# Output units of a group started inside the group: lightning attention with an ACT-snake MLP on one core

## Chip, core and metric

The kernel runs on one core of a Trainium2 chip. The metric is the device time of one execution in microseconds; the time before is the median of three runs, 215.41 us (215.19 to 215.55). One further execution was taken by the hardware profiler. Its own time was 215.56 us, and every duration below is from it, in us from the start of its span.

## What is computed

A causal linear attention with decay (4 batches, 8 heads, 768 positions, head size 64), whose output, as 3072 tokens of 512 columns, goes through an MLP: `h = x @ w_in` (2048 columns), `g = h + sin(alpha h)^2 / alpha`, `out = g @ w_out`.

```python
for b in range(nb):                      # blocks of 64 positions
    intra = einsum('bhic,bhjc->bhij', qb, kb) * Dmask
    intra = einsum('bhij,bhjd->bhid', intra, vb)
    inter = einsum('bhid,bhde->bhie', qb * lam_pow, kv_state)
    out[:, :, sl] = intra + inter
    kv_state = lam_block * kv_state + einsum('bhsd,bhse->bhde', kb * rev_pow, vb)
x = out.transpose(0, 2, 1, 3).reshape(3072, 512)
h = x @ w_in
s = sin(alpha * h)
g = h + s * s / (alpha + 1e-09)
result = g @ w_out
```

## The kernel before

**Tiling.** The 768 positions are cut into NT = 6 chunks of 128. A group g is the MLP of chunk g for all four batches, 512 tokens. The attention of chunk g+1 runs inside the loop of group g, so that its matmuls, its VectorE work and its loads lie between the MLP's.

**The loop.** `for g in range(1, NT + 1)` (L615) has 16 steps i. Each step does, in this order: the loads and transposes that `feed(g)` lists for i; `hidden(g, i)`, which is four matmuls of 128x512 (L402) into a PSUM bank, then the sine on ScalarE (L405) and, where `squarer` says ScalarE, the square (L408); the attention parts that `slots(g)` lists for i; `run(1)`, which takes one unit from the list `behind`; `finish(g, i)`, which is the square on VectorE where `squarer` says so (L416) and then `gall[:, i] = s2 * r + h` from the bank (L417). Group 6 has no hidden parts; it only empties `behind`. At the very end `project_halves` computes the last row block.

**Units.** The second matmul, `g @ w_out`, has four row blocks m (one batch each), and each is four parts of four matmuls (`project`, L427): 16 units for a group, 12 for the last, whose fourth block is `project_halves`. Part p reads the columns f = 4p to 4p+3 of `gall[g]`. Before the change a group's units are queued behind its loop (L636), so they run within the next group's steps, one to a step. Part 0 of a block opens a PSUM bank (L424): for groups 1 to 3 always bank 3 (`OB`), for groups 4 and 5 banks 3 and 4 in turn. Part 3 ends with `store`: a copy from the bank to memory on chip, by VectorE for groups 1 to 3 (L434) and by ScalarE otherwise (L436), and a store on SP's queue (L438).

**Which steps run a unit.** Group 1 starts with seven units of group 0 left, and runs one at i = 0, 1, 2, 3, 5, 8 and 9 (L631). From group 2 on each step runs one.

**Attention parts in a group.** `states` (64 small matmuls, L329) with `update(t, 0)` at step KV and `update(t, 1)` one step later; an update is eight VectorE instructions (L311) and four casts on POOL (L315). `scores` (L348) with `masks(t, 0)` at step F, `masks(t, 1)` one later; each is two VectorE instructions (L355). `outputs` (L366, L374) with `leave(t, 0)` at step O, `leave(t, 1)` one later; each is two VectorE instructions (L382) that write `xt`, the next group's input. KV, F, O are 7, 10, 13 in group 1 and 4, 8, 12 in the others; the last chunk has no `update(t, 1)`.

**What sets the order.** The schedule is manual: each engine runs its instructions in the order in which the program issues them, and waits on semaphores where data or a buffer is not free. Hidden parts rotate over banks 0, 1, 2 (`HB`), so hidden i waits for `finish` of i - 3. Banks 4 to 7 are the attention's. Loads with a cast to bf16 (`pair_load`: k, q and v of two batches) are issued by POOL, which also makes `kdec` (L208) and the casts of L315. Transposes by DMA (`turn_by_dma`) and the stores share SP's queue.

Of the kernel before, what the change touches and what calls it, by code (L numbers as in the profile page):

```python
# [15 lines left out]
def kernel(  # L16
# [14 lines left out]
    B, H, S, D = q.shape  # L31
    T = 128
    NT = S // T
# [156 lines left out]
    V, G, A = nc.vector, nc.gpsimd, nc.scalar  # L190
# [7 lines left out]
    def new_xt(t):  # L198
        xt[t] = xtp.tile([P, NDC, GRP], BF16, name="xt")
# [189 lines left out]
    def squarer(g, f):  # L389
        if g == 0:  # L390
            return V if f in (1, 3, 5, 7, 9, 11) else A
        if g == 1:
            return V if f in (2, 5, 8, 11) else A
        return A

    H0 = (0, 1, 2, 3, 5, 6, 7, 0, 1, 2, 5, 0, 1, 2, 0, 1)
# [1 line left out]
    def hidden(g, f):  # L398
        hps = bank("hps", H0[f] if g == 0 else (2, 4, 5)[f] if g == 1 and f < 3 else HB[(16 * g + f + 1) % 3])
        w = w_in_sb[f // 4]  # L400
        for c in range(NDC):
            nc.tensor.matmul(out=hps[:], lhsT=w[:, c, (f % 4) * P:(f % 4 + 1) * P],  # L402
                             rhs=xt[g][:, c, :], start=(c == 0), stop=(c == NDC - 1))
        s_sb = mlps.tile([P, GRP], BF16, name="s_sb")
        nc.scalar.activation(out=s_sb[:], in_=hps[:], func=ACTF.Sin, scale=alpha_sb[:, f:f + 1])  # L405
        s2 = mlps.tile([P, GRP], BF16, name="s2")
        if squarer(g, f) is A:
            nc.scalar.activation(out=s2[:], in_=s_sb[:], func=ACTF.Square)  # L408
        elif squarer(g, f) is G:
            nc.gpsimd.tensor_tensor(out=s2[:], in0=s_sb[:], in1=s_sb[:], op=ALU.mult)  # L410
        hps_of[g, f] = (hps, s_sb, s2)

    def finish(g, f):
        hps, s_sb, s2 = hps_of.pop((g, f))
        if squarer(g, f) is V:
            nc.vector.tensor_tensor(out=s2[:], in0=s_sb[:], in1=s_sb[:], op=ALU.mult)  # L416
        nc.vector.scalar_tensor_tensor(out=gall[g][:, f, :], in0=s2[:], scalar=r_sb[:, f:f + 1],  # L417
                                       in1=hps[:], op0=ALU.mult, op1=ALU.add)
# [3 lines left out]
    def project(g, m, part):  # L422
        if part == 0:
            ops_of[g, m] = bank("ops", (OB, AB[3], 0, 1)[m] if g == 0 else AB[0] if g > NT - 3 and m % 2 else OB)  # L424
        ops = ops_of[g, m]
        for f in range(4 * part, 4 * part + 4):
            nc.tensor.matmul(out=ops[:], lhsT=gall[g][:, f, m * P:(m + 1) * P],  # L427
                             rhs=w_out_sb[part][:, f % 4, :],
                             start=(f == 0), stop=(f == NFC - 1))

    def store(g, m):
        o_sb = outp.tile([P, DM], FP32, name="o_sb")
        if 0 < g < NT - 2:
            nc.vector.tensor_copy(out=o_sb[:], in_=ops_of.pop((g, m))[:])  # L434
        else:
            nc.scalar.copy(out=o_sb[:], in_=ops_of.pop((g, m))[:])  # L436
        row = m * S + g * T
        nc.sync.dma_start(out=out[row:row + T, :], in_=o_sb[:])  # L438

    def project_halves(g, m):  # L440
        for n in range(2):
            cols = slice(n * DM // 2, (n + 1) * DM // 2)
            ps = bank("hps", HB[n])
            for f in range(NFC):
                nc.tensor.matmul(out=ps[:, 0:DM // 2], lhsT=gall[g][:, f, m * P:(m + 1) * P],  # L445
                                 rhs=w_out_sb[f // 4][:, f % 4, cols],
                                 start=(f == 0), stop=(f == NFC - 1))
            o_sb = outp.tile([P, DM], FP32, name="o_sb")
            nc.scalar.copy(out=o_sb[:, 0:DM // 2], in_=ps[:, 0:DM // 2])
            row = m * S + g * T  # L450
            nc.sync.dma_start(out=out[row:row + T, cols], in_=o_sb[:, 0:DM // 2])
# [79 lines left out]
    def queue_units(g, order):  # L531
        for m, part in order:
            def unit(g=g, m=m, part=part):
                project(g, m, part)
                if part == 3:
                    store(g, m)
            behind.append(unit)

    def run(n):
        for _ in range(min(n, len(behind))):  # L540
            behind.pop(0)()
# [40 lines left out]
    def slots(g):  # L582
        t = g + 1
        d = {i: [] for i in range(NFC)}
        if g == 1:
            at = dict(KV=7, F=10, O=13)
            d[1] += [(states1, 1, 0, 6)]
            d[3] += [(states1, 1, 1, 6)]
        else:
            at = dict(KV=4, F=8, O=12)  # L590
        d[at["KV"]] += [(states, t), (update, t, 0)]
        d[at["KV"] + 1] += [(update, t, 1)]
        d[at["F"]] += [(scores, t), (masks, t, 0)]
        d[at["F"] + 1] += [(masks, t, 1)]
        d[at["O"]] += [(outputs, t), (leave, t, 0)]
        d[at["O"] + 1] += [(leave, t, 1)]
        return d

    def feed(g):
        t = g + 1  # L600
        d = {i: [] for i in range(NFC)}
        if g == 1:
            d[2] += [(turn_by_dma, 2, 0)]
            d[4] += [(pair_ready, 2, 1)]
            d[5] += [(turn_by_dma, 2, 1)]
        if t + 1 < NT:
            d[5 if g == 1 else 2] += [(new_chunk, t + 1), (pair_load, t + 1, 0)]
            d[7 if g == 1 else 4] += [(pair_load, t + 1, 1)]
            d[12] += [(turn_by_dma, t + 1, 0)]
            d[13] += [(pair_ready, t + 1, 0)]  # L610
            d[14] += [(turn_by_dma, t + 1, 1)]
            d[15] += [(pair_ready, t + 1, 1)]
        return d

    for g in range(1, NT + 1):  # L615
        if g < NT:
            gall[g] = gbp.tile([P, NFC, GRP], BF16, name="gall")
        at = slots(g) if g + 1 < NT else {}
        fd = feed(g) if g + 1 < NT else {}
        if g + 1 < NT:  # L620
            new_xt(g + 1)
        for i in range(NFC):
            if g == NT and not behind:
                break
            for a in fd.get(i, []):
                a[0](*a[1:])
            if g < NT:
                hidden(g, i)
            for a in at.get(i, []):
                a[0](*a[1:])  # L630
            if g > 1 or i in (0, 1, 2, 3, 5, 8, 9):  # L631
                run(1)
            if g < NT:
                finish(g, i)
        if g < NT:
            queue_units(g, [(m, part) for m in range(B - 1 if g == NT - 1 else B) for part in range(4)])  # L636
    project_halves(NT - 1, B - 1)


# [28 lines left out]
```

## Time and profile before

| what | value |
|---|---|
| median of three runs | 215.41 us |
| the profiled execution, its own time | 215.56 us |
| its span | 213.8 us |
| instructions | 4810 |
| one hidden or one unit, start to next start on TensorE | 0.86 us |
| L417, one | 0.744 us |
| L405, one | 0.685 us |
| L408, one | 0.630 us |
| L434, one | 0.692 us |
| load of k, q, v from POOL, issue to landing, median | 10.0, 12.9, 12.5 us |
| store of a row block, issue to landing, median | 2.2 us |

The profile has a page of totals and views of the trace. Busy shares are of the span of 213.8 us, or of the stretch named. A matmul's end is modelled, so starts are compared with starts. The tail after the last hidden part is 52 matmuls of L427 (12 units and the last unit of group 4) from 195.76 on the chain of waits, 11.22 us, and the 32 half-width matmuls of `project_halves`, 3.51 us. The DMA engines are busy for nine tenths or more of nearly every slice until about 117 us, and little from then on.

### The profile page before, as it was taken

How to read it: one execution, taken by the hardware profiler on the slowest of the kernel's cores; microseconds unless marked ns; L12 is line 12 of the kernel's file. 1: busy time of each engine (PE TensorE's matmuls, PEld its weight loads, DVE VectorE, ACT ScalarE, POOL GpSimd, SP SyncE). 2: the span in 40 equal slices, each digit the busy share in tenths (PEclk: the TensorE clock that was granted, in tenths of full speed). 3: DMA queues.
4: the chain of work that ended last, by engine and by line, in shares of the span. 5: the costliest groups of instructions: out<-in, count | busy, mean ns of one | idle time of the engine just before them, and what ended most of it. 6: DMA issues, size and time to landing. Idle time of an engine off the chain costs nothing.

```text
span 213.8 us, 4810 instructions
## 1 busy us (share of the span) xinstructions
PE 201.2 (94%) x1953; PEld 99.5 (47%) x1953; DVE 138.5 (65%) x260; ACT 139.6 (65%) x225; POOL 100.1 (47%) x104
## 2 busy tenths in 40 slices
PE   7679998999997879999999999999999999999993
PEld 2444444654443534446444446444446444444452
DVE  6675986774699957995757977648768544444000
ACT  4695979506776677666676764777765778888121
POOL 8999979985499994899001950003100000000000
PEclk9999999999999999999999999999999999999999
DMA  5999999999999999999999016711101001110212
GB/s 103 154 161 206 205 162 180 186 177 154 181 196 185 159 167 138 170 139 120 178 145 198 6 52 112 136 49 52 49 3 52 35 14 49 49 49 5 98 51 98
DMA packets 99814, 24.70 MB, mean 116 GB/s; under 512 B 91968, under 2 KB 96848, under 8 KB 99792
## 3 DMA queue, kind: packets, MB, share of 16 engines
q0 software_dynamic: 77040, 13.37, 87.0%
q1 hardware_dynamic: 21568, 10.76, 24.7%
q10 hardware_dynamic: 1184, 0.27, 0.6%
q8 instruction: 15, 0.25, 0.5%
q14 instruction: 7, 0.06, 0.1%
HBM read 27.28 MB, written 6.29 MB: 157 GB/s over the span
## 4 chain that ended last, share of the span: by engine, by line
PE 75%; DVE 8%; DMA 7%; POOL 5%; ACT 1%; issue 1%; ACTq 0%; POOLq 0%; DVEq 0%
PE ops L427 37%; PE hps L402 30%; DMA w_out<-in_moe_w_out_dram 7%; DVE gall L417 3%; DVE S L311 2%; PE hps L445 2%; POOL kn L101 1%; PE O_ps L366 1%; PE KV_ps L329 1%; POOL qn L101 1%; DVE xt L382 1%; DVE STm L355 1%; POOL vn L101 1%; PE O_ps L374 1%; PE F_ps L348 1%
## 5 line engine op out<-in xcount | busy, mean ns | idle before, releaser
L402 PE MATMUL hps<-xt,w_in 128*128 128x512 bf16 x384 | 96.7, 380 | 3.3 <-DVE xt L382 1.6
L417 DVE SCALAR_TENSOR_TENSOR gall<-s,r_sb,hps 128x512 bf16<-128x512 bf16 x96 | 70.8, 744 | 43.5 <-ACT s L408 43.0
L405 ACT ACTIVATE s_sb<-hps,alpha_sb 128x512 bf16<-128x512 f32 x96 | 65.6, 685 | 50.8 <-PE hps L402 49.8
L427 PE MATMUL ops<-w_out,gall 128*128 128x512 bf16 x368 | 92.5, 380 | 0.5 <-DMA w_out<-in_moe_w_out_dram 0.5
L402 PEld LDWEIGHTS <-w_in 128*128 128x128 bf16 x384 | 36.9, 98 | 47.7 <-issue 4.0
L408 ACT ACTIVATE s<-s_sb 128x512 bf16<-128x512 bf16 x86 | 54.1, 630 | 2.7
L427 PEld LDWEIGHTS <-gall 128*128 128x128 bf16 x368 | 34.6, 98 | 41.2 <-issue 1.4
L315 POOL CAST sbd<-S 64x512 bf16<-64x512 f32 x36 | 22.6, 627 | 45.9 <-DVE S L311 44.4
L208 POOL TENSOR_TENSOR kdec<-kn,R 128x1024 bf16<-128x1024 bf16 x12 | 22.7, 1899 | 1.9 <-DMA kn<-in_k_dram 1.2
L311 DVE SCALAR_TENSOR_TENSOR S<-S,L,KV_ps 128x128 f32<-128x128 f32 x64 | 17.3, 343 | 0.2 <-PE KV_ps L300 0.2
L101 POOL DMA_DIRECT2D kn<-in_k_dram x13 | 14.9, 1148 | 0.3 <-issue 0.3
L101 POOL DMA_DIRECT2D qn<-in_q_dram x13 | 14.4, 1107 | 0.0
L101 POOL DMA_DIRECT2D vn<-in_v_dram x12 | 14.1, 1179 | 0.1
L382 DVE TENSOR_TENSOR xt<-O_ps,Etab 128x512 bf16<-128x512 f32 x16 | 10.3, 684 | 2.5 <-PE O_ps L374 2.5
L436 ACT COPY o_sb<-ops 128x512 f32<-128x512 f32 x11 | 6.3, 574 | 8.5 <-PE ops L427 8.5
L434 DVE COPY o_sb<-ops 128x512 f32<-128x512 f32 x12 | 8.3, 692 | 4.9 <-PE ops L427 4.9
L274 DVE TENSOR_TENSOR STm<-F_ps,C 128x512 bf16<-128x512 f32 x16 | 10.1, 683 | 1.9 <-PE O_ps L285 1.1
L355 DVE TENSOR_TENSOR STm<-F_ps,C 128x512 bf16<-128x512 f32 x16 | 10.3, 683 | 0.0
L456 PE MATMUL hps<-fill 128*128 128x256 bf16 (+1 forms) x32 | 7.9, 369 | 1.5 <-DVE fill L122 1.5
L247 ACT COPY QKT<-T_ps 128x512 bf16<-128x512 bf16 x8 | 4.5, 584 | 1.9 <-PE T_ps L245 1.9
L416 DVE TENSOR_TENSOR s<-s_sb 128x512 bf16<-128x512 bf16 x10 | 4.6, 462 | 1.3 <-ACT s_sb L405 1.3
L292 DVE TENSOR_TENSOR xt<-O_ps,Etab 128x512 bf16<-128x512 f32 x7 | 4.6, 685 | 1.1 <-PE O_ps L285 1.1
(73 smaller groups left out, 95.3 us busy)
## 6 DMA issues: line engine op xcount, KB each, us to landing
out_dram<-o_sb SPq DMA_DIRECT2D x23, 256.0 KB, 2.2
vn<-in_v_dram POOLq DMA_DIRECT2D x12, 256.0 KB, 12.5
kn<-in_k_dram POOLq DMA_DIRECT2D x10, 256.0 KB, 10.0
qn<-in_q_dram POOLq DMA_DIRECT2D x10, 256.0 KB, 12.9
w_out<-in_moe_w_out_dram POOLq DMA_DIRECT2D x4, 512.0 KB, 15.4
w_in<-in_moe_w_in_dram POOLq DMA_DIRECT2D x3, 512.0 KB, 12.2
w_in<-in_moe_w_in_dram POOLq DMA_DIRECT2D x2, 256.0 KB, 8.0
kn<-in_k_dram POOLq DMA_DIRECT2D x3, 128.0 KB, 5.9
```

Of the source, the lines that this page charges most:

```text
L101: nc.gpsimd.dma_start(out=dst[t][:, b0:b1, :, :].rearrange("p b h e -> p (b h) e"), in_=src[b0:b1, :, t * T:(t + 1) * T, :].rearrange("b h ...
L208: nc.gpsimd.tensor_tensor(out=kdec[t][:, b0:b1, :, :], in0=kn[t][:, b0:b1, :, :], in1=R[:].unsqueeze(1).unsqueeze(3).broadcast_to([P, b1 - ...
L274: nc.vector.tensor_tensor(out=st[:, hd], in0=Fb[hd], in1=C0[:, hd], op=ALU.mult)
L311: nc.vector.scalar_tensor_tensor(out=S[:, bs, hp, :], in0=old[:, bs, hp, :], scalar=decay[:, hp:hp + 1], in1=ps[:, :, hp, :], op0=ALU.mult ...
L315: nc.gpsimd.tensor_copy(out=dst[halves(hd), bs, :, hd, :], in_=S[halves(hd), bs, :, :])
L355: nc.vector.tensor_tensor(out=st[:, hd], in0=att["F"][pr, hd], in1=C64[:, hd].unsqueeze(1).broadcast_to([P, 2, HP, D]), op=ALU.mult)
L382: nc.vector.tensor_tensor(out=xview(t)[:, 2 * pr:2 * pr + 2, blk, :, :], in0=att["O"][pr, blk], in1=Eb, op=ALU.mult)
L402: nc.tensor.matmul(out=hps[:], lhsT=w[:, c, (f % 4) * P:(f % 4 + 1) * P], rhs=xt[g][:, c, :], start=(c == 0), stop=(c == NDC - 1))
L405: nc.scalar.activation(out=s_sb[:], in_=hps[:], func=ACTF.Sin, scale=alpha_sb[:, f:f + 1])
L408: nc.scalar.activation(out=s2[:], in_=s_sb[:], func=ACTF.Square)
L417: nc.vector.scalar_tensor_tensor(out=gall[g][:, f, :], in0=s2[:], scalar=r_sb[:, f:f + 1], in1=hps[:], op0=ALU.mult, op1=ALU.add)
L427: nc.tensor.matmul(out=ops[:], lhsT=gall[g][:, f, m * P:(m + 1) * P], rhs=w_out_sb[part][:, f % 4, :], start=(f == 0), stop=(f == NFC - 1))
```

## The change

Four edits, all in groups 1 and later:

- `squarer`: in group 1 the squares of f = 8 and f = 11 are ScalarE's (L408) where they were VectorE's (L416). f = 2 and 5 stay on VectorE.
- `feed`: in group 1 the second pair of loads of chunk 3 is issued at step 8, not 7. On POOL's queue its three loads come behind the four casts of `update(2, 0)`, where they came ahead of them.
- `own`: two units of a group, parts 0 and 1 of its block 0, are queued within its own loop: in group 1 at i = 10 and 12, in the others at 14 and 15. Group 1 runs its seven units of group 0 at the same steps as before and its own two at 10 and 12. After its loop it queues the rest and runs one more, part 2 of block 0, ahead of group 2's first hidden part.
- the steps that run a unit: group 2 runs none at i = 0. With part 3 of block 0 then at i = 1, block 1 runs at i = 2 to 5, block 2 at 6 to 9, block 3 at 10 to 13, and group 2's own two units at 14 and 15. Groups 3 and 4 start with part 2 at i = 0 and part 3 at i = 1 and go on in the same way; so does group 5. The tail has 10 units.

```diff
         if g == 1:
-            return V if f in (2, 5, 8, 11) else A
+            return V if f in (2, 5) else A
...
             d[5 if g == 1 else 2] += [(new_chunk, t + 1), (pair_load, t + 1, 0)]
-            d[7 if g == 1 else 4] += [(pair_load, t + 1, 1)]
+            d[8 if g == 1 else 4] += [(pair_load, t + 1, 1)]
...
+        own = {10: (0, 0), 12: (0, 1)} if g == 1 else {14: (0, 0), 15: (0, 1)}
         for i in range(NFC):
             if g == NT and not behind:
                 break
+            if g < NT and i in own:
+                queue_units(g, [own[i]])
             for a in fd.get(i, []):
                 a[0](*a[1:])
             if g < NT:
                 hidden(g, i)
             for a in at.get(i, []):
                 a[0](*a[1:])
-            if g > 1 or i in (0, 1, 2, 3, 5, 8, 9):
+            if i not in ((4, 6, 7, 11, 13, 14, 15), (0,))[g - 1] if g < 3 else True:
                 run(1)
             if g < NT:
                 finish(g, i)
         if g < NT:
-            queue_units(g, [(m, part) for m in range(B - 1 if g == NT - 1 else B) for part in range(4)])
+            queue_units(g, [(m, part) for m in range(B - 1 if g == NT - 1 else B) for part in range(4)][2:])
+            if g == 1:
+                run(1)
```

## The prediction

> **What bounds the kernel now.** I read first the engines' busy shares and the granted clock in 40 slices, then the chain of waits that ended last, then busy time by stretch, and last the order of time around each place that the diff touches. "Hidden" below is one chunk f of L402 (four matmuls), "unit" four matmuls of L427.
>
> ```profile
> PE 201.2 (94%) x1953; PEld 99.5 (47%) x1953; DVE 138.5 (65%) x260; ACT 139.6 (65%) x225; POOL 100.1 (47%) x104
> ...
> PEclk9999999999999999999999999999999999999999
> ```
>
> ```profile
> 60.00:76.00 16.00, 12.56 (x265) 6.89 (x265) 15.62 (x36) 11.18 (x19) 15.54 (x17) 1.00 1.88 165
> 76.00:107.00 31.00, 30.99 (x353) 15.30 (x353) 22.91 (x44) 20.69 (x33) 22.18 (x22) 1.00 2.05 152
> 107.00:138.00 31.00, 31.00 (x354) 15.21 (x352) 22.98 (x44) 21.11 (x33) 8.63 (x10) 1.00 0.80 111
> ```
>
> The columns of the last three lines are stretch, length, busy PE, PEld, DVE, ACT, POOL, clock, DMA share, GB/s. From 76 us on (groups 2 and later) TensorE has no pause, so there every microsecond in which it waits is added to the end. From 60 to 76 us (the second half of group 1) it is busy for 12.56 of 16 us, and VectorE for 15.62: here VectorE is the bound. The chain of waits says the same:
>
> ```profile
> 66.31 0.34 DVE s L416
> ...
> 66.67 1.41 DVE gall L417 x2
> ...
> 71.13 0.34 DVE s L416
> ...
> 74.76 1.21 DVE xt L382 x2
> ...
> 76.01 1.02 PE hps L402 x4
> ```
>
> The rows at L416 are the two squares that the diff takes off VectorE, and the chain comes back to TensorE at 76.01, where hidden(2,0) waited for L382. The order of time shows what closes and opens the one bank of the units, bank 3:
>
> ```profile
> 86.28 1.03 PE L427 MATMUL ops<-w_out,gall 128*128 128x512 bf16 x4
> ...
> 87.14 1.03 PE L402 MATMUL hps<-xt,w_in 128*128 128x512 bf16 x4
> 87.16 2.15 DVE L311 SCALAR_TENSOR_TENSOR S<-S,L,KV_ps 128x128 f32<-128x128 f32 x8
> ...
> 88.00 1.03 PE L427 MATMUL ops<-w_out,gall 128*128 128x512 bf16 x4
> ...
> 89.23 1.40 DVE L417 SCALAR_TENSOR_TENSOR gall<-s,r_sb,hps 128x512 bf16<-128x512 bf16 x2
> ...
> 93.91 1.28 DVE L355 TENSOR_TENSOR STm<-F_ps,C 128x512 bf16<-128x512 f32 x2
> ...
> 95.68 1.03 PE L427 MATMUL ops<-w_out,gall 128*128 128x512 bf16 x4
> ```
>
> ```profile
> 106.89 1.03 PE L402 MATMUL hps<-xt,w_in 128*128 128x512 bf16 x4
> ...
> 107.09 0.69 DVE L434 COPY o_sb<-ops 128x512 f32<-128x512 f32 x1 [0.46 <-PE ops L427]
> ...
> 107.83 1.02 PE L427 MATMUL ops<-w_out,gall 128*128 128x512 bf16 x4
> ```
>
> A unit or hidden starts 0.86 after the one before (88.00 - 87.14). In the second fence the last unit of a row block is copied out by VectorE at 107.09, and the first unit of the next block, which reuses the bank, starts 0.05 after the copy's end, at 107.83 instead of 106.89 + 0.86 = 107.75: **0.08 lost although VectorE was free.** So a unit that opens bank 3 starts 0.69 + 0.05 = 0.74 after its copy starts, and the copy can start 1.06 after the closing unit (97.41 to 98.47 in the order of time). With one hidden between (1.73 from unit to unit) that loses 0.08; with an attention part between it loses nothing. Before, the copies of groups 2 to 4 stand at i = 3, 7, 11, 15, and states, scores and outputs come at i = 4, 8, 12: three of four are covered. The copies of group 1's blocks fall in group 2, and so on.
>
> **The change, part by part.**
>
> *Two squares (f = 8, 11 of group 1) to ScalarE.* On VectorE each fills 0.36 of the chain (66.31 to 66.67, 71.13 to 71.50). A ScalarE square takes 0.63 (L408); ScalarE is busy 11.18 of 16 us there and idle 1.04 before the sine at 63.61, so the first lies in a pause, and the second ends (below) before its reader.
>
> *Three units of group 1 inside group 1.* They are 3 x 0.86 = 2.59 of TensorE work that leaves later places: group 2 runs 15 units instead of 16 (0.86), the tail 10 instead of 12 (1.73). Groups 3 to 5 keep 16. What they cost in group 1 I walk through. The scores end at 66.70; unit (0,0) 66.70; hidden 11 at 67.58 (0.88 after attention, as 84.54 to 85.42); hidden 12 at 68.44; unit (0,1) 69.31; hidden 13 at 70.17; outputs 71.03. VectorE without the squares: L417 twice from 66.31 (1.33), masks 67.64 (1.19), L417 68.83, masks 69.49 (1.20), L417 twice from 70.69; the square of f = 11 ends at 67.58 + 1.06 + 0.72 + 0.63 = 69.99, in time. They end at 72.01, but L382 can start only 1.52 after outputs start (99.14 to 100.66): 72.55. Then 1.20 to the L417, 0.66 to the second L382 at 74.41, which ends 1.28 later at 75.69; hidden(2,0) starts 0.05 behind, at 75.74. The third unit lies at 74.46 to 75.33, in the pause that was 1.57 long. So group 1 takes in all three units and still ends **0.27 earlier**. Ends: 0.73 (both squares in full) and -0.5 (each new unit delays a hidden that VectorE then waits for). Gain so far 0.27 + 0.86 + 1.73 = 2.86.
>
> *What moves with them.* Group 2 now starts with unit (0,2) done, so its block ends, and so the copies L434, fall at i = 1, 5, 9, 13 in place of 3, 7, 11, 15; groups 3 to 5 the same. Every opening unit (i = 2, 6, 10, 14) then has one hidden alone between it and the closing one, and the copy stands in VectorE's order behind the attention work of its slot:
> - i = 5, groups 2 and 3: the copy stands behind update(t, 1), eight L311. In the positions of before those run from 87.16 to 89.23; the copy 89.23, the unit of i = 6 at 89.23 + 0.74 = 89.97 instead of 88.00: **1.97 of TensorE standing still**, with all later hiddens queued behind that unit. Group 3's rows (L311 at 118.12, next L417 at 120.19) give the same. Ends 1.6 and 2.3 each. Group 4 has no update at i = 5: 0.08.
> - i = 9, groups 2 to 4: the masks at 93.91 end at 95.11; the copy then; the unit at 95.85 instead of 95.68: 0.17 each.
> - i = 13, groups 2 to 4: the second L382 pair (102.52 + 1.21 = 103.73), so 104.47 against 104.30: 0.17 each.
> - i = 1: 0.08 in groups 3 and 4. In group 2 two hiddens come first, without a unit, and the copy stands behind the L417 of f = 0, which starts 2.44 after its hidden (76.01 to 78.45), so at 78.18; copy 78.85, unit at 79.59 instead of 79.20: 0.39.
> - The 0.08 at the three old boundaries (i = 15 to 0) goes. In group 5 ScalarE copies and blocks alternate between two banks: nothing.
>
> Sum: group 2 0.39 + 1.97 + 0.17 + 0.17 = 2.70; group 3 2.39; group 4 0.50; less 0.24: **5.35**. Ends for the small ones together (1.65): 0.8 and 3.0.
>
> *The tail.* Unit (0,3) of group 5 needs L417 of f = 15, which ends at 197.93, 2.3 after hidden 15's successor starts (195.59). It had three units in front, now two: its last weights would load 0.21 before 197.97. Cost 0.15, ends 0 and 0.25.
>
> *The pair of loads behind four casts.* POOL is free at 62.86; four casts at 0.655 (5.24 for 8) end at 65.5, so the three loads start there and not at 62.81: 2.7 later. kn, qn and vn landed about 8.9, 13.2 and 15.8 after issue (DMA answers for these windows). vn was there at 80.9, with states(3) from 83.87. Now it lands by 83.6 if all 2.7 is handed on, and states(3), at 83.05, reads that pair half-way, at 83.4. The queue was full from 63 to 73 us, so I take 0; ends 0 and 1.0. The decay on POOL behind kn ends by 76.3, the transposes on SP's queue behind qn by 88, scores(3) not before 92: free. On SP one store now stands between two pairs of transposes: one issue (0.6 at 57.12), wanted a group later. POOL's remaining four casts feed the next group's outputs: free.
>
> *The clock.* Between 60 and 76 us TensorE paused for 0.6, 0.7, 0.6 and 1.57, and the granted clock was 1.00; I take nothing for it. The Trainium skill, "TensorE: Matmul & The Clock Gate", section "HAM oscillation", holds pauses under some 3.4 us harmless, which 1.97 is; its section "A second HAM failure mode: psum-queue depth-cycling" says short pauses between groups that cycle through PSUM banks can make the clock fall again and again. By the first rule the sum stays, by the second it is the clock rival below; the trace bears out the first.
>
> Total: -2.86 + 5.35 + 0.15 = +2.64. The profiled execution took 215.56 (span 213.8 and 1.8 around it): 218.2. The median of the runs shown, 215.41, is 0.15 less: **218.1**.
>
> **The rivals.**
> 1. *The opening unit doesn't wait for the copy* (a second bank, or a copy that VectorE reaches before update). For it: in groups 4 and 5 L424 alternates banks. Against: for groups 1 to 3 L424 gives bank 3 to every block, and L434's copy comes after L311 in the slot. Without the two pauses at i = 6: 218.1 - 3.9 = **214.2**, faster; it decides once those two lose together less than 1.3. 5%.
> 2. *The loads come late:* states(3) waits for vn, up to 1.0, and group 1 gives nothing back (0.8 worse): **219.9**. For it: vn's margin is 3 us against 2.7 of delay; against: a full DMA queue hides a late issue. 12%.
> 3. *The pauses are half as long* (VectorE gets ahead while TensorE stands, or update starts sooner): 218.1 - 2.0 = **216.1**, still slower; against it: all eight L311 wait for states, which TensorE itself runs. 6%.
> 4. *The clock falls* at each long pause: if two units and two hiddens (3.46) run at half pace twice, 6.9 more, **225.0**. Against: clock 1.00 in every stretch shown. 2%.
>
> **How the numbers follow.** The forecast has 75%, its own range 217.4 to 218.9. What a measurement can tell from no change is 0.2%, 0.43 us here. Slower: forecast, rivals 2 and 4, and nearly all of 3, 75 + 12 + 2 + 4 = 93%; same 2% (the rest of 3); faster 5%. The range of 8 in 10 takes in half of rivals 2 and 3 and the bounds of the copies: 216.7 to 219.4.
>
> **What would show it.** Right: in groups 2 and 3 one pause of TensorE of about 2 us each, ended by L434, behind eight L311; hidden(2,0) near 75.7; a tail of 40 + 4 L427 matmuls; pauses of 0.1 to 0.4 before the other opening units. Wrong: units at i = 6 back to back with their hidden, a DMA wait at L329, a clock under 0.95, or a group 1 that ends later than 76.0.

## The result, and the profile after

The changed kernel took 218.38 us, median of 4 runs (218.02 to 218.68), against 215.41 before: ratio 1.0138, 95% interval 1.0118 to 1.0158. It is slower, by 3.0 us. The profiled execution took 218.57, its span 216.8.

From the page after, busy shares and the granted clock in 40 slices:

```profile
PE 200.6 (93%) x1929; PEld 99.6 (46%) x1953; DVE 137.3 (63%) x258; ACT 140.6 (65%) x227; POOL 99.6 (46%) x104
...
PEclk9999999999999999999999999999999999999999
```

TensorE has as much to do as before in a span that is 3.0 longer. Where it stands still is in the busy time by stretch (columns as in the prediction):

```profile
60.00:76.00 16.00, 14.41 (x273) 7.83 (x265) 14.44 (x33) 11.33 (x19) 13.11 (x16) 1.00 1.76 176
76.00:107.00 31.00, 28.26 (x338) 13.93 (x340) 22.93 (x45) 19.83 (x31) 23.89 (x23) 1.00 1.98 154
107.00:138.00 31.00, 28.53 (x339) 14.21 (x342) 20.68 (x41) 19.14 (x30) 8.64 (x10) 1.00 0.75 94
```

From 60 to 76 us TensorE gained 1.85 of work (12.56 to 14.41), and VectorE is no longer full. In the two stretches behind, where it had no pause at all, it now misses 2.7 and 2.5. The chain of waits through the middle of group 2 says who holds it:

```profile
86.37 0.07 DVE gall L417
86.44 0.51 issue
86.95 2.15 DVE S L311 x8
89.09 0.61 DVE o_sb L434
89.70 0.04 issue
89.75 1.02 PE ops L427 x4
```

The eight L311 of the second update, then the copy L434, then the unit that reuses bank 3. In the order of time on TensorE:

```profile
86.93 1.03 PE L402 MATMUL hps<-xt,w_in 128*128 128x512 bf16 x4
89.75 1.02 PE L427 MATMUL ops<-w_out,gall 128*128 128x512 bf16 x4 [1.78 <-DVE o_sb L434]
...
120.14 1.03 PE L402 MATMUL hps<-xt,w_in 128*128 128x512 bf16 x4
123.11 1.02 PE L427 MATMUL ops<-w_out,gall 128*128 128x512 bf16 x4 [1.95 <-DVE o_sb L434]
```

The opening unit would have started 0.86 after its hidden, at 87.79 and 121.00. It started 1.96 and 2.11 later. Before, units stood at these places without a gap.

The whole difference, by starts on TensorE in the two profiles:

| stretch | before | after | change | forecast |
|---|---|---|---|---|
| start to states(2) in group 1 | 60.14 | 59.80 | -0.34 | 0 |
| states(2) to hidden(2,0) | 15.87 | 16.48 | +0.61 | -0.27 |
| group 2, to hidden(3,0) | 30.88 | 32.65 | +1.77 | +1.84 |
| group 3 | 30.95 | 33.36 | +2.41 | +2.31 |
| group 4 | 30.91 | 31.29 | +0.38 | +0.42 |
| group 5, to the tail's first unit | 26.84 | 26.76 | -0.08 | -0.08 |
| tail, to `project_halves` | 11.23 | 9.52 | -1.71 | -1.58 |
| rest | 6.98 | 6.94 | -0.04 | 0 |
| sum | 213.8 | 216.8 | +3.0 | +2.64 |

Two rows are off, both in group 1. In the first stretch both kernels run the same instructions, and over the twelve profiles of this document it lies between 59.71 and 60.47, so its -0.34 is not put down to the change. In the second the order of time after has:

```profile
66.86 0.45 PE L348 MATMUL F_ps<-QKT 64*64 64x64 bf16 x32 [1.43 <-DMA QKT<-qn]
...
76.28 1.89 PE L402 MATMUL hps<-xt,w_in 128*128 128x512 bf16 x8 [0.25 <-DVE xt L382]
```

Half-way through its scores TensorE waited 1.43 for the transposed q of chunk 2's second pair. Before, that place waited 0.59 for L311:

```profile
66.36 0.44 PE L348 MATMUL F_ps<-QKT 64*64 64x64 bf16 x31 [0.59 <-DVE S L311]
```

### The profile page after: what moved, and what is told of

It is laid out like the page before. It is cut to its first block, busy times and chain, and to the rows that moved or that the text cites. A ratio compares the mean times of both kernels' runs of the same rounds, so it can differ in the third digit from the quotient of the medians.

```text
span 216.8 us, 4787 instructions
## 1 busy us (share of the span) xinstructions
PE 200.6 (93%) x1929; PEld 99.6 (46%) x1953; DVE 137.3 (63%) x258; ACT 140.6 (65%) x227; POOL 99.6 (46%) x104
## 4 chain that ended last, share of the span: by engine, by line
PE 66%; DMA 10%; DVE 7%; POOL 5%; SPq 4%; issue 3%; ACT 2%; ACTq 0%; POOLq 0%; DVEq 0%
PE ops L427 32%; PE hps L402 25%; DMA w_out<-in_moe_w_out_dram 7%; DVE S L311 4%; SPq L222 4%; DMA QKT<-qn 3%; PE O_ps L366 2%; PE hps L445 2%; POOL kn L101 1%; POOL qn L101 1%; DVE xt L382 1%; PE F_ps L348 1%; PE O_ps L374 1%; POOL vn L101 1%; ACT s_sb L405 1%
## 5 line engine op out<-in xcount | busy, mean ns | idle before, releaser
L417 DVE SCALAR_TENSOR_TENSOR gall<-s,r_sb,hps 128x512 bf16<-128x512 bf16 x96 | 70.9, 743 | 52.2 <-ACT s L408 51.6
L402 PE MATMUL hps<-xt,w_in 128*128 128x512 bf16 x375 | 95.7, 379 | 1.0 <-DVE xt L292 0.3
L427 PE MATMUL ops<-w_out,gall 128*128 128x512 bf16 x353 | 90.1, 379 | 6.2 <-DVE o_sb L434 4.0
L408 ACT ACTIVATE s<-s_sb 128x512 bf16<-128x512 bf16 x88 | 55.4, 630 | 2.8
L315 POOL CAST sbd<-S 64x512 bf16<-64x512 f32 x36 | 22.1, 614 | 48.4 <-DVE S L311 46.9
L208 POOL TENSOR_TENSOR kdec<-kn,R 128x1024 bf16<-128x1024 bf16 x12 | 22.7, 1900 | 4.3 <-DMA kn<-in_k_dram 3.6
L311 DVE SCALAR_TENSOR_TENSOR S<-S,L,KV_ps 128x128 f32<-128x128 f32 x64 | 17.4, 341 | 0.4 <-PE KV_ps L300 0.2
L434 DVE COPY o_sb<-ops 128x512 f32<-128x512 f32 x12 | 8.2, 682 | 1.0 <-PE ops L427 0.9
L456 PEld LDWEIGHTS <-fill 128*128 128x128 bf16 x32 | 2.9, 112 | 3.9 <-issue 2.0
```

The costliest lines, as they stand in the source:

```text
L208: nc.gpsimd.tensor_tensor(out=kdec[t][:, b0:b1, :, :], in0=kn[t][:, b0:b1, :, :], in1=R[:].unsqueeze(1).unsqueeze(3).broadcast_to([P, b1 - ...
L311: nc.vector.scalar_tensor_tensor(out=S[:, bs, hp, :], in0=old[:, bs, hp, :], scalar=decay[:, hp:hp + 1], in1=ps[:, :, hp, :], op0=ALU.mult ...
L315: nc.gpsimd.tensor_copy(out=dst[halves(hd), bs, :, hd, :], in_=S[halves(hd), bs, :, :])
L456: nc.tensor.matmul(out=ps[:, 0:cols], lhsT=fill[:, 0:P], rhs=fill[:, 0:cols], start=True, stop=True)
```

## The experiments

The kernel before ran beside each on the same chip: medians 215.45 (17 runs) for `e1`, `e2`, `e3` and `e5`, 215.37 (18, on another chip) for `e6` to `e9`, and 215.32 (7) for `e10` and `e11`.

**1. The copy ahead of the attention part** (`e3_copy_first`). In steps 5, 9 and 13 the unit is issued ahead of that step's VectorE work.

```diff
+            early = g > 1 and i in (5, 9, 13)
+            if early:
+                run(1)
             for a in at.get(i, []):
                 a[0](*a[1:])
-            if i not in ...:
+            if early:
+                pass
+            elif i not in ...:
                 run(1)
```

> The changed kernel with the unit of steps 5, 9 and 13 (groups 2 and later), and so its copy, issued ahead of that step's attention part; TensorE's order is unchanged, on VectorE the copy stands ahead of update(t,1), of masks(t,1) and of the second leave. Theory: the pauses at step 6 go from 1.8 to 1.95 down to 0.08, but L417 of f = 5 ends 0.15 later than hidden 8 wants it, so 0.23 stays; steps 10 and 14 go from 0.17 to 0.08. Sum about -4.0: 214.4, below the kernel before. Rival (VectorE is short of time in these slots, so what the copy gains the updates lose): L311 ends 0.6 later, hiddens wait for L417 instead, and the time is 217 or more.

Measured 214.02 (213.89 to 214.94), ratio to before 0.9947 [0.9933, 0.9962]: 4.4 below the changed kernel and 1.4 below the kernel before. In its order of time the copy stands ahead of the eight L311, and the unit follows its hidden with 0.09 lost:

```profile
86.38 1.03 PE L402 MATMUL hps<-xt,w_in 128*128 128x512 bf16 x4
...
87.33 1.02 PE L427 MATMUL ops<-w_out,gall 128*128 128x512 bf16 x4
```

```profile
86.58 0.69 DVE L434 COPY o_sb<-ops 128x512 f32<-128x512 f32 x1
87.19 2.15 DVE L311 SCALAR_TENSOR_TENSOR S<-S,L,KV_ps 128x128 f32<-128x128 f32 x8
```

The updates lose 0.6 and nobody waits for them but hidden 8: 0.14 (90.05 instead of 89.91). The rival falls. Of the 4.6 by which the profiled span is shorter (212.2 against 216.8), 0.56 lies ahead of hidden(2,0), since the transposed q was in time in this execution; the rest is the 4.0 that was expected. The copy's place in VectorE's order was the loss.

**2. Another engine for the one copy** (`e2_block1_act`).

```diff
-        if 0 < g < NT - 2:
+        if 0 < g < NT - 2 and m != 1:
             nc.vector.tensor_copy(out=o_sb[:], in_=ops_of.pop((g, m))[:])
```

> The changed kernel with ScalarE copying out row block 1 of groups 1 to 3 (the copies at step 5 of groups 2 to 4), all other copies as they are. Theory (the pause at step 6 is the copy standing behind eight L311 on VectorE): the pauses of 1.8 to 1.95 in groups 2 and 3 shrink to about 0.44 (sine and square of hidden 5 end 2.41 after its start, the copy 0.57 later), group 4 goes from 0.08 to 0.44; sum -2.7, so 215.7. Rival (the bank or the moved phase itself costs, whichever engine copies): 218.4.

Measured 215.07, median of 12 (214.74 to 217.72), ratio 1.0004 [0.9982, 1.0026]. In group 2's order of time:

```profile
89.14 1.03 PE L402 MATMUL hps<-xt,w_in 128*128 128x512 bf16 x4
90.35 1.02 PE L427 MATMUL ops<-w_out,gall 128*128 128x512 bf16 x4 [0.18 <-ACT o_sb L436]
```

The unit would have started at 90.00, so 0.35 is lost, and the same in group 3: 3.4 less for the two than in the changed kernel. Group 4 loses 0.35 where it lost 0.08. That makes 3.1 of the 3.3 by which the median fell; 2.7 was expected. The bank and the phase are those of the changed kernel; only the queue that the copy stands in differs.

**3. The phase alone** (`e9_phase_only`): no unit in its own group, no square or load moved.

```diff
-            if g > 1 or i in (0, 1, 2, 3, 5, 8, 9):
+            if i in (0, 1, 2, 3, 5, 8, 9) if g == 1 else g > 2 or i > 1:
                 run(1)
```

> The kernel before, with group 2 running no unit at steps 0 and 1 and nothing else changed: same squares, same loads, no unit inside its own group; two units more end in the tail, and row blocks end at steps 5, 9, 13 and 1. Theory (the phase of the copies alone makes the loss): pauses of 1.97 at step 6 of groups 2 and 3, 0.08 to 0.17 at the other openings: 2.31 + 2.39 + 0.50 - 0.24 = 4.96, so 220.4. Rival (the loss came from the units inside the group, from ScalarE's two squares or from the loads): 215.4 to 216.

Measured 224.56 (222.83 to 225.15), ratio 1.0411 [1.0378, 1.0443]. The two long pauses are there without the rest of the change:

```profile
88.69 1.02 PE L427 MATMUL ops<-w_out,gall 128*128 128x512 bf16 x4 [1.92 <-DVE o_sb L434]
...
123.01 1.02 PE L427 MATMUL ops<-w_out,gall 128*128 128x512 bf16 x4 [2.17 <-DVE o_sb L434]
```

By starts they lost 2.08 and 2.33. The phase alone makes more than the whole loss; the rival falls. The size was wrong by 4.2. One part of that is a wait I had overlooked. Group 1's last two units now run at steps 0 and 1 of group 3, while `finish(3, 0)` wants to write the `gall` buffer that they read (there are two), and the copy is queued behind it. The order of time at that boundary:

```profile
111.61 0.75 DVE L417 SCALAR_TENSOR_TENSOR gall<-s,r_sb,hps 128x512 bf16<-128x512 bf16 x1 [2.25 <-PE ops L427]
112.27 0.68 DVE L434 COPY o_sb<-ops 128x512 f32<-128x512 f32 x1
...
113.01 1.02 PE L427 MATMUL ops<-w_out,gall 128*128 128x512 bf16 x3 [0.65 <-DVE o_sb L434]
```

That is 0.81 (113.01 against 111.33 + 0.86 = 112.19) where I had 0.08, in groups 3 and 4 alike, and in group 5, where I had nothing: 2.27 in all, so 222.7. Two of the six executions took 222.83 and 222.91. The other four took 224.5 to 225.2, and the rest of it is in the last section.

**4. The units without the phase** (`e6_aligned`): three units in group 1, none in later groups' own loops, and group 2 starts its 13 at step 3, so blocks end at 3, 7, 11, 15 again.

```diff
-        own = {10: (0, 0), 12: (0, 1)} if g == 1 else {14: (0, 0), 15: (0, 1)}
+        own = {10: (0, 0), 12: (0, 1)} if g == 1 else {}
...
-            if i not in ((4, 6, 7, 11, 13, 14, 15), (0,))[g - 1] if g < 3 else True:
+            if i not in ((4, 6, 7, 11, 13, 14, 15), (0, 1, 2))[g - 1] if g < 3 else True:
...
-... for part in range(4)][2:])
+... for part in range(4)][2 if g == 1 else 0:])
```

> The changed kernel with three units of group 1 inside group 1, but no own units in later groups, and group 2 running its 13 units from step 3 on, so that row blocks end at steps 3, 7, 11 and 15 as in the kernel before. Theory (the moved units are a gain, only the phase of the copies costs): no pause at step 6, the short ones only at the group boundaries; group 2 is three units shorter (2.59), but its first four hiddens follow each other without units and hidden 3 waits about 0.65 for L417 of f = 0; hidden(2,0) at about 75.7. 215.4 - 0.3 - 2.59 + 0.65 = 213.2. Rival (the units removed leave group 2 bound by ScalarE and VectorE, so their time is not won): 214.4 or more, no better than the squares alone.

Measured 213.33 (212.98 to 214.03), ratio 0.9908 [0.9894, 0.9923]: this version beats both kernels, by 2.0 and 5.0. TensorE's waits from 55 us on, as the view lists them (us in total, times, longest):

```profile
PE F_ps L348 <- DMA QKT<-qn: 1.6, 1, 1.6
PE hps L402 <- DVE gall L417: 0.5, 1, 0.5
PE hps L402 <- DVE xt L382: 0.3, 1, 0.3
PE ops L427 <- issue: 0.2, 1, 0.2
```

No wait for a copy is in the list; by starts 0.09 is still lost at each group boundary, where the kernel before loses 0.08. The price is one wait of 0.49 for L417 of f = 0.

**5. The squares** alone on the kernel before (`e5_squares_only`), and taken back out of experiment 1 (`e8_copy_first_squares_back`).

```diff
-            return V if f in (2, 5, 8, 11) else A
+            return V if f in (2, 5) else A
```

> The kernel before with the two squares of group 1 on ScalarE and nothing else. Theory (VectorE bounds group 1 from 61 us on): hidden(2,0) starts 0.73 earlier, 75.3, and the time is 0.7 lower, 214.7. Rival (something else is late there, the transposes or ScalarE): 215.2 to 215.4.

> e3_copy_first with the two squares of group 1 back on VectorE. Theory (with the three units in group 1 TensorE and the outputs set the pace, so the squares are nearly free): hidden(2,0) 0.2 later, 214.2. Rival (the squares are worth as much here as alone, 0.7 to 1.0): 214.8 to 215.0.

Alone: 214.43 (214.35 to 214.53), ratio 0.9957 [0.9945, 0.9969], so 1.0 rather than 0.7. In the profiles 0.55 of it lies between states(2) and hidden(2,0) (15.32 against 15.87), although the scores waited 1.76 for the transposed q; another 0.43 lies ahead of states(2), where nothing was edited. Taken back out: 214.46 (214.13 to 216.81) against 214.02, so 0.4 rather than 0.2; the intervals, 0.9940 to 0.9981 and 0.9933 to 0.9962, overlap. So the squares pay alone. Whether they are worth less beside the units, because both fill the same pauses of group 1, is not shown. The units were not run without the squares; with them and in the old phase (experiment 4) they came to 213.33, another 1.1 less.

**6. The loads** back at step 7, in the changed kernel (`e1_loads_back`) and in experiment 1 (`e7_copy_first_loads_back`).

```diff
-            d[8 if g == 1 else 4] += [(pair_load, t + 1, 1)]
+            d[7 if g == 1 else 4] += [(pair_load, t + 1, 1)]
```

> The changed kernel with the second pair of loads of chunk 3 back at step 7, ahead of the four casts. In the changed profile TensorE waited 1.43 us inside the scores of group 1 for the transposed q (landed at 66.73), and hidden(2,0) started at 76.28 where 75.74 was forecast. Theory (that wait is an accident of the DMA queue in one execution, the load move has nothing to do with it, since the transposes are issued before the moved loads): time stays at 218.4, within 0.4, and the transposes' landing varies from profile to profile by about 1 us. Rival (the moved loads, once they are put back, free the transposes): the wait of 1.43 goes, hidden(2,0) at about 75.4, 217.5. Both: the two pauses of 1.8 to 1.95 at step 6 of groups 2 and 3 stay.

> e3_copy_first with the second pair of loads back at step 7. Theory (the place of these loads decides nothing, the late transposes of some executions are the queue's own scatter): 214.0, within 0.3. Rival (the loads issued at 62.8 run beside the transposed q that the scores of group 1 want, and make it late more often): median 214.5 or more, with single runs above 215; hidden(2,0) after 76.3 in the profile.

The first took 218.77 (218.01 to 219.94), which against 218.02 to 218.68 decides nothing; its scores waited 2.05 for the transposed q, so the wait is not made by moving the loads. The second took 214.04 (213.81 to 215.18) against 214.02: the move is worth nothing that can be measured.

**7. The transposes** of chunk 2's second pair ahead of a store on SP's queue, in experiment 4 (`e10_aligned_turn_early`) and in the changed kernel (`e11_after_turn_early`).

```diff
-            d[2] += [(turn_by_dma, 2, 0)]
+            d[2] += [(turn_by_dma, 2, 0), (turn_by_dma, 2, 1)]
...
-            d[5] += [(turn_by_dma, 2, 1)]
```

> e6_aligned with the transposes of chunk 2's second pair issued at step 2 of group 1, behind those of the first pair and ahead of the output store that stood between them on SP's queue. Theory (the late transposed q in group 1 is SP's queue: the store's issue of 0.6 and its transfer stand in front of the transposes): they start 0.6 to 0.7 earlier, the wait of 1.55 inside the scores shrinks to 1.0 or less, median 212.8. Rival (the transposes wait for their loads or for the DMA queue, not for their place on SP): no change, 213.3.

> The changed kernel with the same one move of the transposes. Theory: group 1's scores no longer wait 1.43 for the transposed q; hidden(2,0) goes from 76.3 towards 75.7, median 217.8. Rival: 218.4 as the changed kernel. Both: the pauses of about 1.9 at step 6 of groups 2 and 3 stay.

The changed kernel with this took 217.83 (217.71 to 217.95), ratio 1.0117 [1.0102, 1.0132], 0.55 less. Its scores wait for L311 as those of the kernel before do, and from states(2), at 59.78, to group 2's start it takes 15.64, where the forecast had 15.60:

```profile
66.00 0.44 PE L348 MATMUL F_ps<-QKT 64*64 64x64 bf16 x31 [0.59 <-DVE S L311]
...
75.42 1.89 PE L402 MATMUL hps<-xt,w_in 128*128 128x512 bf16 x8 [0.26 <-DVE xt L382]
```

In experiment 4 the wait for the transposes goes as well, but the median stays at 213.28 (213.26 to 213.56; ratio 0.9910 [0.9893, 0.9926]), as the rival had it. I had overlooked that the scores then wait 0.57 for L311. Its four runs lie within 0.3, where those of experiment 4 spread over 1.05.

## Why the prediction held

**The pauses at step 6** (forecast 1.97 each): 1.96 and 2.11. Experiments 1 and 2 remove them by changing nothing but where the copy stands, and 3 brings them about without the rest of the change. This is shown.

**The short pauses.** Step 2 of group 2: 0.40 (unit at 80.12 instead of 79.72) for 0.39. Steps 10 and 14 there: 0.16 and 0.15 (97.58 for 97.42, 106.34 for 106.19) for 0.17. Step 2 of group 3: 0.08 for 0.08.

**The work taken out of group 2 and the tail** came as forecast, 0.86 and 1.73. The tail's charge of 0.15 for the late L417 didn't arise: 9.52 against 11.23 - 1.73 = 9.50.

**Group 1 is the step that was mis-sized**: "group 1 takes in all three units and still ends 0.27 earlier". Counted from states(2) it ended 0.61 later, and hidden(2,0), at 76.28, lies behind the 76.0 that the prediction had named as a sign of being wrong. The walk let L311 open the second half of the scores, at 66.36, and never asked where the transposed q was. In the profile of before it had landed by 64.5 (issued at 59.19, 5.3 to landing), ahead of that half; in the changed kernel's it landed at 66.7 (59.56, 7.2). SP's queue, before and then after:

```profile
57.81 1.28 SPq L222 DMA_TRANSPOSE QKT<-kn  x1
59.19 1.39 SPq L222 DMA_TRANSPOSE QKT<-qn  x1
```

```profile
57.21 2.25 SPq L222 DMA_TRANSPOSE QKT<-kn  x1
59.56 1.31 SPq L222 DMA_TRANSPOSE QKT<-qn  x1
```

In the profiled executions in which it was there in time (experiments 1, 7 twice, and the second of 6), hidden(2,0) starts 15.63 or 15.64 after states(2); the walk has 75.74 - 60.14 = 15.60. So the units are absorbed and the squares shorten group 1 as worked out, and the term was short of one wait. It stands in seven of the twelve profiles taken: with 1.06 to 2.05 in the changed kernel and in `e1_loads_back`, `e2_block1_act`, `e5_squares_only`, `e6_aligned` and `e8_copy_first_squares_back`, and with 0.64 in `e9_phase_only`. In all seven the transpose of k just ahead on SP's queue took 1.81 to 2.25; in the profile of before, experiment 1 and the second of 6 it took 1.28 or 1.29. What makes it short or long from execution to execution stays open. An earlier place on SP's queue helped in `e11_after_turn_early`: the transpose of k took 2.30 there, q landed by 64.4 all the same, and the four runs lie below all four of the changed kernel, though the two intervals overlap. In `e10_aligned_turn_early` it took 1.31, so that profile decides nothing.

Over all of group 1 the forecast missed by 0.54, since the six profiles with a wait of more than 1 also reach states(2) earlier (59.71 to 59.88) than before, experiment 1 and the second of 6 do (60.09 to 60.14). The other rows of the table missed by -0.18 together, so that the total came within 0.4 owes a little to luck.

**The loads**: vn's margin held, states(3) waited for nothing. kn came late instead: POOL's L208 waited 2.45 for it, until 75.59, and ended at 77.49 where 76.3 was forecast; nobody waited for L208. The move of the loads is not shown to be the cause: with the loads at their old place L208 waited 2.58 in `e1_loads_back` and 2.43 in `e5_squares_only`.

**The rivals.** The unit that doesn't wait: no, it waits as L424 says. Its price was about right, though: without the two long pauses experiment 1, which shortens some of the small ones too, took 214.0, the forecast for the rival 214.2. Late loads: no. Half pauses: no. The clock: not in the changed kernel's profile, but see below.

## What to carry to other kernels

Moving work by a slot or two moves every later handover of a buffer: for each one, look at what stands ahead of the releasing instruction in its engine's queue at the new place. A copy that frees a bank for the engine at the bound belongs ahead of longer work that nobody awaits so soon. Where a pause is to be filled, list everything that can end it, not only what ended it in one profile.

## What the runs showed of the hardware

In two profiles the granted clock fell to half in the loop, behind a pause of TensorE. The stretches of `e9_phase_only` behind the pause of 2.17 that ended at 123.01, one microsecond each (clock is the third figure from the right):

```profile
123.00:124.00 1.00, 0.99 (x5) 0.48 (x5) 1.00 (x2) 0.00 (x0) 0.93 (x2) 1.00 0.18 68
124.00:125.00 1.00, 1.00 (x5) 0.36 (x3) 0.28 (x1) 0.00 (x0) 0.94 (x1) 0.57 0.52 195
125.00:126.00 1.00, 1.00 (x4) 0.35 (x3) 0.00 (x0) 0.44 (x1) 1.00 (x2) 0.50 0.00 0
126.00:127.00 1.00, 1.00 (x3) 0.30 (x2) 0.05 (x1) 0.88 (x2) 1.00 (x1) 0.50 0.00 0
127.00:128.00 1.00, 1.00 (x5) 0.40 (x3) 0.69 (x1) 0.00 (x0) 0.82 (x1) 0.73 0.00 0
```

What is missing from 1.00 adds up to 1.70, which is 3.4 at half rate; from hidden 7 to the scores it took 4.37 (123.87 to 128.24) where the same steps before took 2.68 (88.87 to 91.55). The profile of `e2_block1_act` has the same behind its wait of 1.87 in the scores: 0.50 from 68 to 71 us, 1.71 missing, and its execution was the slowest of twelve, 217.72. Behind pauses of 1.78 and 1.95 (the changed kernel), 1.92 (the first of `e9_phase_only`) and 2.05 (`e1_loads_back`) the clock stayed at 1.00.

The profile of `e9_phase_only` has one more fall, near its start (the second of the 40 slices):

```profile
PEclk9799999999999999999999699999999999999999
```

By microseconds it is 0.54, 0.50, 0.50 and 0.75 from 8 to 12 us, again 1.71 missing, behind pauses of 1.17 and 1.04 with 0.61 of work between them. In the profile of before the pauses there were 0.29 and 1.05, and the clock was 1.00.

One such fall takes 0.008 from the mean clock of a whole execution (1.7 of 220 us). In `e9_phase_only` the mean was 0.999 and 1.0 in the two executions of 222.8 and 222.9, 0.991 in the three of 224.5 to 224.9, and 0.984, two falls, in the profiled one of 225.15. The mean doesn't say where a fall lies or what it costs: in `e8_copy_first_squares_back` 0.992 goes with 216.81 and with 214.46, and one execution of the changed kernel had 0.992 and took 218.20, less than the median. So a pause of the length that the change makes can cost 1.7 more. It didn't in the changed kernel's profile, but nothing that the prediction had worked out ruled it out.

The Trainium skill, "TensorE: Matmul & The Clock Gate", section "What's actually happening", gives half rate and a window of about 3.4 us, which both traces bear out (0.50, and 1.70 and 1.71 missing). It asks for at least one idle window of that length before the fall; here pauses of 1.87 and 2.17 were enough, and others as long were not. What decides between them no run here shows. That a pause of 1.97 lies under some 3.4 was therefore no safe ground for taking nothing for the clock in the prediction.
